# Relative-bias attention and a snake-activation MLP in one kernel: numerators and divisions in two groups per head pair, one transpose of x per pair, other loads and planner figures

## The chip, the cores and the metric

The kernel runs on one core of a Trainium2 chip. A core has a matrix engine (TensorE, PE; its weight loads are shown as PEld), a vector engine (VectorE, DVE), a scalar engine (ScalarE, ACT), GpSimd (POOL) and SyncE (SP), which run separate instruction streams and wait for each other through semaphores, and 16 DMA engines. The metric is the device time of one execution in microseconds.

## The reference

```python
def _attn_ref(q, k, v, bias_table):        # q, k, v: (8, 8, 576, 64); bias_table: (32, 8)
    scores = scale * np.matmul(q, k.transpose(0, 1, 3, 2))
    ...
    bias = bias_table[bucket]              # bucket: a function of |i - j|, 31 from some distance on
    scores = scores + bias.transpose(2, 0, 1)[None, :, :, :]
    scores = scores - np.max(scores, axis=-1, keepdims=True)
    attn = np.exp(scores)
    attn = attn / (np.sum(attn, axis=-1, keepdims=True) + 1e-09)
    return np.matmul(attn, v).astype(np.float32)

def _moe_ref(x, w_in, w_out, alpha):       # x: (4608, 512), w_in: (512, 2048), w_out: (2048, 512)
    h = x @ w_in
    s = np.sin(alpha * h)
    g = h + s * s / (alpha + 1e-09)
    return (g @ w_out).astype(np.float32)

def reference(**kwargs):
    ...
    x = np.ascontiguousarray(attn_out.transpose(0, 2, 1, 3)).reshape(B * S, H * D)
    return _moe_ref(x=x, **moe_kwargs)
```

## The kernel before

**Attention** goes through the 8 sequences t and, in each, the 4 head pairs p. k and q are wanted with the head dimension on the partitions: for t = 0 and 1 they are loaded by rows into the buffer of tile g (`natural`, L259), turned on PE by identity (`turn`, L366) and copied to kT and qT (L396); for later t POOL casts them into HBM (`stage`, L238) and SP's DMA transposes fetch them (L245). kL (L417) holds the last 64 keys of both heads of a pair in the two diagonal corners, so that one matmul with all 128 rows serves both heads. A pair has five score tiles of up to 1024 columns: X (last 64 keys and last 64 queries, L601 and L608) and four of 256 by 256 blocks (L698); one small tile S per sequence serves the last keys against the last queries (L575). ScalarE takes exp of each tile into a u (L544). The bias is a product afterwards: exp(bias - bias at distance 31) stands in m2 and mt, built at the start by selecting table rows with a matmul (`mask`, L459), and DVE multiplies the tiles near the diagonal by it (L616, L618, L709, L713, L717).

**Numerators and divisions.** `av_task` (L626) makes one unit of 128 queries for both heads: 9 matmuls (L639, L643) into 130 columns of one bank of PSUM (tile av), column 64 of each head being the sum of the exps. Three such slots of the bank are used in turn. `norm` then does a reciprocal (L653) and a multiply (L657) per unit into tile xp. A pair has five units; the one of the last 64 queries comes first. `xtr` (L735) turns xp into xT by two DMA transposes on SP (four chunks of 128 rows, then 64 rows).

**The MLP** goes through 9 blocks of 512 tokens. `moe_in(b)` (L747) has 8 steps of 1024 features: 8 matmuls (L764), two sines (L774), a square (L781) and two fused multiply-adds into g (L788); then 16 pieces of 4 matmuls with w_out (L821), an eviction (L837) and a store for each 128 tokens. A block needs xT of all its tokens. Block t - 1 stands behind pair 1 of sequence t, and block 0 behind pair 0 of sequence 1.

**The order** of each engine's instructions is made in advance: `_Plan` (L60) knows tasks with an engine, a duration, a latency, dependencies, rings of buffers and a priority, plays them through and emits them in the order of its clock. HOP is what passes from one engine to another, LATENCY what an engine's result takes, SWITCH what a change of kind costs. The tasks on the ring `big` (score tiles, masks and moe steps, three PSUM buffers) keep the order in which they were added. POOL's loads keep theirs too: k and q of t = 0 (heads 0 and 1, then the other six), v of t = 0, w_in, k and q of t = 1, v, w_out, then the later sequences.

Of the kernel before, what the change touches and what calls it, by code (L numbers as in the profile page):

```python
# [47 lines left out]
class _Task:  # L48
    def __init__(self, eng, dur, emit, deps=(), prio=0, lat=0.0, rings=(), seq=None, name="", mode=None):
        self.eng, self.dur, self.emit = eng, dur, emit  # L50
        self.deps = list(deps)
        self.prio, self.lat, self.rings = prio, lat, list(rings)
        self.mode = mode
        self.seq = seq
        self.name = name
        self.start = None
        self.end = None


class _Plan:  # L60
# [4 lines left out]
    HOP = 0.1  # L65

    LATENCY = {"PE": 0.15, "ACT": 0.1, "DVE": 0.08}
# [19 lines left out]
    def _ready(self, t):  # L87
        r = 0.0
        for d in t.deps:
            if d.end is None:  # L90
                return None
            r = max(r, d.end + self.HOP)
# [11 lines left out]
    def run(self):  # L104
# [9 lines left out]
        while left:  # L114
            moved = False
            nxt = None
            for e, lst in engs.items():
# [13 lines left out]
                if best is not None:  # L131
# [5 lines left out]
                    best.start = now  # L137
# [19 lines left out]
def kernel(  # L157
# [34 lines left out]

    bt = _bucket_table(256)
    cst_np = np.zeros((128, 672), dtype=np.float16)
    for g in range(4):
        for z in range(511 - g):
            cst_np[32 * g + bt[abs(255 - z)], z + g] = 1.0
        cst_np[32 * g:32 * g + 32, 640 + 8 * g:648 + 8 * g] = 1.0
# [10 lines left out]
    xT = sgl.tile([128, NP, NT], F16, name="xT")  # L209
# [5 lines left out]
    t31 = sgl.tile([128, H], F32, name="t31")  # L215
    dtab = sgl.tile([128, H], F32, name="dtab")
# [11 lines left out]
    big, avr, mor = _Ring(3), _Ring(3), _Ring(1)  # L228
# [40 lines left out]

    def load_v(t):  # L270
# [27 lines left out]
    def pre_sp():  # L298
# [3 lines left out]
        nc.sync.dma_start(  # L302
            out=t31, in_=bass.AP(tensor=bias_table.tensor,
                                 offset=bias_table.offset + (NB - 1) * H,
                                 ap=[[0, 128], [1, H]]))
# [31 lines left out]
    def pre_tab():  # L337

        nc.vector.tensor_tensor(out=dtab, in0=tab4, in1=t31, op=ALU.subtract)
        nc.vector.tensor_copy(out=hilo[:, 0, :], in_=dtab)  # L340
        nc.vector.tensor_tensor(out=hilo[:, 1, :], in0=dtab, in1=hilo[:, 0, :], op=ALU.subtract)
# [7 lines left out]
    t_tab = add("SP", 0.9, pre_sp, lat=1.6)  # L349
# [3 lines left out]
    t_al = add("SP", 1.2, pre_sp2, lat=4.0)  # L353
    t_dve0 = add("DVE", 1.5, pre_dve)
    t_bt = add("DVE", 0.7, pre_tab, deps=[t_tab, t_sp0], prio=-3)
    t_alpha = add("DVE", 0.4, pre_alpha, deps=[t_al])
# [9 lines left out]
    def turn(t, p):  # L366

        for kind in range(2):
# [3 lines left out]
            def e_pe(kind=kind, cell=cell, first=first):  # L372
                if first:

                    avs["t"] = ps.tile([128, 512], F32, name="av", tag="av", bufs=1)
                    avs["n"] = 0
                    s = cell["t"] = avs["t"].bitcast(F16)
                else:
                    s = cell["t"] = ps.tile([128, 512], F32, name="mo", tag="mo", bufs=1).bitcast(F16)
                r = nat[t]["n"]  # L380
                for j in range(NL):
# [8 lines left out]
            def e_cp(kind=kind, cell=cell, first=first):  # L390
                dst = (kTs, qTs)[kind][t % 2][:, p, 0:S].rearrange("d (r j) -> d r j", j=NL)
                src = ap(cell["t"], 0, [[1, NR], [NR, NL]])
                if first:
                    nc.scalar.activation(out=dst, in_=src, func=AF.Copy)
                else:
                    nc.vector.tensor_copy(out=dst, in_=src)  # L396
            users = []
            a = add("PE", 0.6, e_pe, deps=[T_nat[t][p][kind], t_sp0], prio=-0.5 if t else -2 if p == 0 else 0,
                    rings=[(avr, users)] * 3 if first else [(mor, users)], mode="full",
                    name=f"turn{t}.{p}.{kind}")  # L400
            if first:
                c = add("ACT", 0.7, e_cp, deps=[a], prio=-1, name=f"turn{t}.{p}.{kind}c")
            else:
                c = add("DVE", 0.6, e_cp, deps=[a], prio=-2, name=f"turn{t}.{p}.{kind}c")
# [3 lines left out]
        corners(t, p, 1, [T_kT[t][p], t_dve0])  # L408

    def corners(t, p, n, deps):  # L410
        def emit():
            for a_ in range(2):
                r = slice(64 * a_, 64 * a_ + 64)
                dst = kLs[t % 2][r, p:p + n, 64 * a_:64 * a_ + 64]
                src = kTs[t % 2][r, p:p + n, 512:576]
                if n == 1:
                    nc.vector.tensor_copy(out=dst, in_=src)  # L417
                else:
                    nc.sync.dma_start(out=dst, in_=src)
        c = add("DVE" if n == 1 else "SP", 0.25 if n == 1 else 0.9, emit, deps=deps, prio=-1,  # L420
                name=f"kL{t}.{p}")
        if n > 1:
            c.lat = 3.0
        T_kL[t][p:p + n] = [c] * n
# [4 lines left out]
    def load_nat(t):  # L429
        kq = ((0, k), (1, q))  # L430

        def one(emit, dur):
            first = not made
            made.append(add("GQ", dur, emit, lat=3.0, seq="GQ",
                            rings=[(gr, nat_users[t])] if first else []))
            return made[-1]
        made = []
        parts = [(0, 2), (2, 6)] if t == 0 else [(0, 8)]
        for h0, n in parts:
            got = [one(natural(src, t, kind, h0, n), 0.45 * n) for kind, src in kq]  # L440
            for p in range(h0 // 2, (h0 + n) // 2):
                T_nat[t][p] = got

    load_nat(0)
    T_v[0] = add("GQ", 5.0, load_v(0), deps=[t_dve0], lat=3.0, seq="GQ")
# [31 lines left out]
    avs = {}  # L477
    T_mt = []

    def masks_tail():  # L480

        for pp in range(2):
            cell = {}

            def g_mm(pp=pp, cell=cell):
                if "t" not in avs:
                    avs["t"] = ps.tile([128, 512], F32, name="av", tag="av", bufs=1)
                    avs["n"] = 0
                cell["t"] = avs["t"][:, 0:384].rearrange("p (a b) -> p a b", a=2)
# [11 lines left out]
            a = add("PE", 0.4, g_mm, deps=list(T_m2), prio=-1, rings=[(avr, users)] * 3,  # L501
# [9 lines left out]
    def later_loads(t):  # L511
        pre_k = last_qk[t - 2] if t >= 2 else []
        pre_v = last_av[t - 2] if t >= 2 else [t_dve0]
        if t == 1:
            for j in range(4):
                T_win.append(add("GQ", 2.5, w_in_load(j), lat=2.0, seq="GQ"))
        if t < TN:
            load_nat(t)
        else:
# [7 lines left out]
            corners(t, 0, NP, [c] + pre_k)  # L527
        T_v[t] = add("GQ", 5.0, load_v(t), deps=pre_v, lat=3.0, seq="GQ")
        if t == 1:
            for i in range(4):  # L530
                T_wout.append(add("GQ", 2.5, w_out_load(i), lat=2.0, seq="GQ"))


    def feed_tile(cell, dur, full, rows, exp_cols, deps_pe, tag, ring=None, kind="u", bufs=NU, home=None):
# [12 lines left out]
        if batch["open"] is not None:  # L547
# [8 lines left out]
        else:  # L556
# [5 lines left out]
        b = add("ACT", 0.05 + exp_cols / 1200.0, e_act, deps=[a], seq="ACT",  # L562
                rings=[(ring or ur, uu)], name=tag + "e", mode="exp")
        users.append(b)
# [5 lines left out]
    def attn_s(t, cell):  # L570
        qT, kL = qTs[t % 2], kLs[t % 2]

        def full(s):
# [3 lines left out]
        a, b = feed_tile(cell, 0.14, full, None, 256, T_kL[t] + T_qT[t], f"S{t}",  # L577
# [13 lines left out]
    def attn_pair(t, p, sc):  # L591
# [12 lines left out]
        def mm_x(s):  # L604
            for c in range(4):
# [5 lines left out]
        ax, bx = feed_tile(cx, 0.36, full_x, mm_x, 1024, kq + [T_kL[t][p]], f"X{t}.{p}")  # L611
# [14 lines left out]
        def av_task(units, part, deps, qc):  # L626


            cell = {}

            def emit():
                if "t" not in avs:
                    avs["t"] = ps.tile([128, 512], F32, name="av", tag="av", bufs=1)
                    avs["n"] = 0
                o = cell["o"] = 130 * (avs["n"] % 3)
                avs["n"] += 1
                av = avs["t"]
                tail, bl = units()
                nc.tensor.matmul(out=av[:, o:o + 130], lhsT=tail, rhs=vt_[:, p, 0:130],  # L639
                                 start=True, stop=True, skip_group_check=True)  # L640
                for a_ in range(2):
                    for c in range(4):
                        nc.tensor.matmul(  # L643
                            out=av[:, o + 65 * a_:o + 65 * a_ + 65],
                            lhsT=bl(a_, c), rhs=vv[:, c, hA + a_, 0:65],
                            start=False, stop=True, skip_group_check=True)

            def norm():
                if "x" not in xcell:
                    xcell["x"] = tp.tile([128, 5, 128], F16, name="xp", tag="xp", bufs=NX)  # L650
                av, x, o = avs["t"], xcell["x"], cell["o"]
                r = tp.tile([128, 2], F32, name="rden", tag="rden", bufs=6)
                nc.vector.reciprocal(  # L653
                    out=r[0:part, 0:2],
                    in_=bass.AP(tensor=av.tensor, offset=av.offset + o + 64,
                                ap=[[av.ap[0][0], part], [65, 2]]))
                nc.vector.tensor_tensor(  # L657
                    out=bass.AP(tensor=x.tensor, offset=x.offset + 128 * qc,
                                ap=[[x.ap[0][0], part], [64, 2], [1, 64]]),
                    in0=bass.AP(tensor=av.tensor, offset=av.offset + o,  # L660
                                ap=[[av.ap[0][0], part], [65, 2], [1, 64]]),
                    in1=bass.AP(tensor=r.tensor, offset=r.offset,
                                ap=[[r.ap[0][0], part], [1, 2], [0, 64]]),
                    op=ALU.mult)
            users = []
            a = add("PE", 0.3, emit, deps=deps + [T_v[t]], prio=1, rings=[(avr, users)],
                    name=f"av{t}.{p}.{qc}", mode="full")
            rings = [(xr, xusers)] if not norm_done else []
            b = add("DVE", 0.4, norm, deps=[a], prio=0, rings=rings, name=f"norm{t}.{p}.{qc}")
# [4 lines left out]
        def units_q4():  # L674
# [3 lines left out]
        a4 = av_task(units_q4, 64, [dx], 4)  # L678
        if "band" in sc:
            a4.deps.append(sc["band"])  # L680
            sc["users"].append(a4)
        else:
            sc["early"].append(a4)
        cx["users"].append(a4)
# [230 lines left out]
```

## Time and profile before

| | us |
|---|---|
| three runs | 430.11, 436.71, 435.34; median 435.34 |
| profiled execution | 435.95, of it the span of the instructions 434.1 |
| mean granted clock | 0.972 |
| PE, DVE, ACT, POOL busy | 386.6, 317.6, 272.9, 74.7 |
| L544 exp, 160 of 128x1024 | 154.7 |
| L764 and L821 matmuls | 134.3 and 132.1 + 15.9 |
| L653 and L657, 160 each | 26.3 and 46.4 |
| L788, L781, L709 | 100.9, 48.9, 43.8 |

All times in views are us from the span's first instruction unless marked ns. A line such as "PE av L639" is an engine, the tile written and the line of the program; "<-" names what ended a wait. A row of the timeline has its start, its length, the engine, the line, the operation, what it writes and reads, and in brackets the idle time before it. In the chain that ended last, PE has 55% of the span and DVE 37%.

### The profile page before, as it was taken

What the parts mean: (1) busy time and instruction counts of PE and PEld (TensorE: products, weight loads), DVE (VectorE), ACT (ScalarE), POOL (GpSimd) and SP (SyncE); (2) the same over time, 40 slices, a digit from 0 to 9 for tenths busy, and PEclk for the clock granted to TensorE, in tenths of its full rate; (3) what the DMA queues carried; (4) which work ended last, traced back from release to release, by engine and by line L of the source; (5) the groups of instructions that cost most, each with busy time, mean ns of one, the idle gap of its engine ahead of it and who ended that gap; (6) DMA issues with size and microseconds to landing.
All of it is one profiled execution on the core that took longest, in us unless ns stands there. A gap on an engine that the chain in (4) does not pass through costs nothing.

```text
span 434.1 us, 9402 instructions
## 1 busy us (share of the span) xinstructions
PE 386.6 (89%) x3848; PEld 206.5 (48%) x3848; DVE 317.6 (73%) x827; ACT 272.9 (63%) x333; POOL 74.7 (17%) x78
## 2 busy tenths in 40 slices
PE   3774778999799899989998999899989999999996
PEld 3653533455345554455445544554455445444442
DVE  4578848877687669866986698768866896399811
ACT  2666516888549784979397948794778486355400
POOL 7526260006100430034003500220000000000000
PEclk9889669999989999999999999999999999999999
DMA  9999999719990799359933994293212101100021
GB/s 117 194 197 171 178 143 154 67 41 107 144 127 31 81 143 113 98 69 156 118 91 55 152 121 107 45 152 63 65 40 53 30 32 40 39 26 0 24 98 73
DMA packets 158463, 40.78 MB, mean 94 GB/s; under 512 B 148052, under 2 KB 153300, under 8 KB 158420
## 3 DMA queue, kind: packets, MB, share of 16 engines
q0 software_dynamic: 98976, 18.35, 54.9%
q1 hardware_dynamic: 59300, 21.66, 26.9%
q8 instruction: 30, 0.49, 0.5%
q10 hardware_dynamic: 144, 0.17, 0.1%
q14 instruction: 13, 0.11, 0.1%
HBM read 36.89 MB, written 16.52 MB: 123 GB/s over the span
## 4 chain that ended last, share of the span: by engine, by line
PE 55%; DVE 37%; issue 4%; DMA 2%; ACT 1%; SPq 0%; DVEq 0%
PE mo L821 17%; DVE g L788 15%; PE big L764 15%; PE av L643 8%; DVE sq L781 7%; PE big L698 5%; DVE xp L657 4%; PE av L639 3%; PE av L821 3%; DVE outs L837 3%; DVE rden L653 2%; DMA xT<-xp 2%; PE big L459 1%; DVE kL L417 1%; PE big L601 1%
## 5 line engine op out<-in xcount | busy, mean ns | idle before, releaser
L544 ACT ACTIVATE u<-big 128x1024 f16<-128x1024 f32 x160 | 154.7, 1022 | 35.2 <-PE big L698 21.7
L774 ACT ACTIVATE s<-big,alphaT 128x512 f16<-128x512 f32 x144 | 90.8, 684 | 87.2 <-PE big L764 87.1
L764 PE MATMUL big<-xT,w_in 128*128 128x512 f16 x576 | 134.3, 387 | 4.8 <-DVE g L788 4.1
L821 PE MATMUL mo<-w_out,g 128*128 128x512 f16 x512 | 132.1, 380 | 6.2 <-DVE g L788 3.5
L788 DVE SCALAR_TENSOR_TENSOR g<-sq,inv_a,big 128x512 f16<-128x512 f16 x144 | 100.9, 744 | 1.7
L764 PEld LDWEIGHTS <-w_in 128*128 128x128 f16 x576 | 57.0, 100 | 74.9 <-issue 11.4
L821 PEld LDWEIGHTS <-g 128*128 128x128 f16 x576 | 50.9, 97 | 67.1 <-issue 10.8
L643 PEld LDWEIGHTS <-u 128*128 128x128 f16 x1280 | 53.3, 99 | 28.8 <-issue 19.8
L781 DVE TENSOR_TENSOR sq<-s 128x1024 f16<-128x1024 f16 x72 | 48.9, 687 | 24.7 <-ACT s L774 24.6
L643 PE MATMUL av<-v,u 128*128 128x65 f16 x1280 | 61.1, 195 | 1.3 <-DVE u L709 1.3
L277 POOL DMA_DIRECT2D v<-in_v_dram x32 | 28.3, 901 | 193.5 <-PE av L643 192.1
L653 DVE RECIPROCAL rden<-av 128x2 f32<-128x2 f32 (+1 forms) x160 | 26.3, 165 | 40.6 <-PE av L643 40.1
L657 DVE TENSOR_TENSOR xp<-av,rden 128x128 f16<-128x128 f32 (+1 forms) x160 | 46.4, 290 | 5.5
L709 DVE TENSOR_TENSOR u<-u,m 128x1024 f16<-128x1024 f16 x64 | 43.8, 684 | 4.9 <-ACT u L544 4.9
L698 PE MATMUL big<-qT,kT 64*128 64x256 f16 x512 | 43.3, 279 | 0.0
L639 PE MATMUL av<-vt,u 128*128 128x130 f16 x128 | 28.7, 224 | 10.0 <-DVE xp L657 9.9
L837 DVE COPY outs<-mo 128x512 f32<-128x512 f32 x32 | 22.0, 687 | 6.8 <-PE mo L821 6.1
L698 PEld LDWEIGHTS <-kT 64*128 64x128 f16 x512 | 19.0, 96 | 16.6 <-issue 13.9
L639 PEld LDWEIGHTS <-u 128*128 128x128 f16 x128 | 12.5, 98 | 9.5 <-issue 3.8
L238 POOL DMA_DIRECT2D staged_q<-in_q_dram x6 | 16.7, 2788 | 0.0
L821 PE MATMUL av<-w_out,g 128*128 128x512 f16 x64 | 15.9, 379 | 0.0
L639 PE MATMUL av<-vt,us 128*128 128x130 f16 x32 | 7.1, 221 | 9.7 <-DVE xp L657 9.4
(56 smaller groups left out, 189.5 us busy)
## 6 DMA issues: line engine op xcount, KB each, us to landing
out_dram<-outs SPq DMA_DIRECT2D x36, 256.0 KB, 2.2
v<-in_v_dram POOLq DMA_DIRECT2D x32, 128.0 KB, 5.6
staged_k<-in_k_dram POOLq DMA_DIRECT2D x6, 576.0 KB, 10.9
staged_q<-in_q_dram POOLq DMA_DIRECT2D x6, 576.0 KB, 17.5
w_in<-in_moe_w_in_dram POOLq DMA_DIRECT2D x4, 512.0 KB, 9.3
w_out<-in_moe_w_out_dram POOLq DMA_DIRECT2D x4, 512.0 KB, 11.4
xT<-xp SPq DMA_TRANSPOSE x64, 4.8
g<-in_k_dram POOLq DMA_DIRECT2D x1, 576.0 KB, 13.5
```

Of the source, the lines that this page charges most:

```text
L544: nc.scalar.activation(out=cell["u"][:, 0:exp_cols], in_=cell["s"][:, 0:exp_cols], func=AF.Exp, scale=0.125)
L639: nc.tensor.matmul(out=av[:, o:o + 130], lhsT=tail, rhs=vt_[:, p, 0:130], start=True, stop=True, skip_group_check=True)
L643: nc.tensor.matmul(out=av[:, o + 65 * a_:o + 65 * a_ + 65], lhsT=bl(a_, c), rhs=vv[:, c, hA + a_, 0:65], start=False, stop=True, skip_grou ...
L657: nc.vector.tensor_tensor(out=bass.AP(tensor=x.tensor, offset=x.offset + 128 * qc, ap=[[x.ap[0][0], part], [64, 2], [1, 64]]), in0=bass.AP ...
L698: nc.tensor.matmul(out=s[:, 512 * a_ + 256 * ci:512 * a_ + 256 * ci + 256], lhsT=kT[r, p, 128 * c:128 * c + 128], rhs=qT[r, p, 256 * w:256 ...
L709: nc.vector.tensor_tensor(out=io, in0=io, in1=m2[:, hA:hA + 2, :], op=ALU.mult)
L764: nc.tensor.matmul(out=cell["h"][:, 512 * i:512 * i + 512], lhsT=w_in16[:, j, 128 * f:128 * f + 128], rhs=xT[:, j, 512 * b:512 * b + 512], ...
L774: nc.scalar.activation(out=cell["s"][:, 512 * i:512 * i + 512], in_=cell["h"][:, 512 * i:512 * i + 512], func=AF.Sin, scale=alphaT[:, f:f ...
L781: nc.vector.tensor_tensor(out=cell["sq"], in0=cell["s"], in1=cell["s"], op=ALU.mult)
L788: nc.vector.scalar_tensor_tensor(out=gcell["g"][:, f, :], in0=cell["sq"][:, 512 * i:512 * i + 512], scalar=inv_a[:, f:f + 1], in1=cell["h" ...
L821: nc.tensor.matmul(out=cell["mo"][:, :], lhsT=gcell["g"][:, f, 128 * a_:128 * a_ + 128], rhs=w_out16[:, f, :], start=(f == 0), stop=(f == ...
L837: nc.vector.tensor_copy(out=cell["o"], in_=cell["mo"][:, :])
```

## The change

Numerators: the units of a pair go in two groups, two units and three (the last 64 queries now with the third and fourth chunk). A group has the whole bank; one reciprocal and one multiply divide it, over all 128 partitions. The ring of three slots becomes a ring of one. x of a pair is turned by one DMA transpose of five chunks, whose last 64 columns, of no meaning, are written over by the next sequence; xT is 64 columns longer.

For t = 0 and 1 kL is no longer made: X and S multiply half the rows at a time. For t = 1, k and q come by 128 rows of the sequence (ten loads in place of two, in runs of 64 elements where there were 384), with five transposes each and a copy in order. For t = 0 the loads are by one, one and two pairs. The selection matrix subtracts row 31 itself, so the table is loaded once and not subtracted. Alpha is loaded after the masks. In sequence 1 block 0 of the MLP stands behind pair 1, and w_in is loaded after k and q. The planner's figures change, an instruction on the same engine no longer waits for the latency, and the exp behind the first of two score tiles issued together is planned from the end of that tile.

```diff
-    HOP = 0.1
-    LATENCY = {"PE": 0.15, "ACT": 0.1, "DVE": 0.08}
+    HOP = 0.04
+    LATENCY = {"PE": 0.17, "ACT": 0.1, "DVE": 0.08}
...
-            r = max(r, d.end + self.HOP)
+            if d.eng == t.eng and d.eng in self.LATENCY:
+                r = max(r, d.start + d.took)
+            else:
+                r = max(r, (d.start + t.after[d] if d in t.after else d.end) + self.HOP)
...
-            cst_np[32 * g + bt[abs(255 - z)], z + g] = 1.0
+            cst_np[32 * g + bt[abs(255 - z)], z + g] += 1.0
+            cst_np[32 * g + NB - 1, z + g] -= 1.0
...
+    def natural_chunk(src, t, kind, c):
+        def emit():
+            nc.gpsimd.dma_start(
+                out=rows_of(t)[:, 5 * kind + c, :].rearrange("p (h d) -> p h d", d=D),
+                in_=bass.AP(tensor=src.tensor, offset=src.offset + t * H * S * D + 128 * c * D,
+                            ap=[[D, 128], [S * D, H], [1, D]]))
...
-        nc.sync.dma_start(
-            out=t31, in_=bass.AP(tensor=bias_table.tensor,
...
-        nc.vector.tensor_tensor(out=dtab, in0=tab4, in1=t31, op=ALU.subtract)
-        nc.vector.tensor_copy(out=hilo[:, 0, :], in_=dtab)
+        nc.vector.tensor_copy(out=hilo[:, 0, :], in_=tab4)
...
+                if t:
+                    for c in range(5):
+                        n = 128 if c < 4 else 64
+                        nc.tensor.transpose(out=s[:, 128 * c:128 * c + n],
+                                            in_=r[0:n, 5 * kind + c, 128 * p:128 * p + 128],
+                                            identity=i_sb[0:n, 0:n])
+                    return
...
-        corners(t, p, 1, [T_kT[t][p], t_dve0])
...
-        parts = [(0, 2), (2, 6)] if t == 0 else [(0, 8)]
+            for h0, n, lat in ((0, 2, 4.0), (2, 2, 5.0), (4, 4, 6.0)):
...
+            got = [[one(natural_tail(src, t, kind), 0.7, 4.0)] for kind, src in kq]
+            for kind, src in kq:
+                got[kind] += [one(natural_chunk(src, t, kind, c), 0.9, 5.0) for c in range(4)]
...
+    t_al = add("SP", 0.5, pre_sp2, deps=T_m2, lat=6.0)
...
+        for load in ((kqs, w_ins, v_s, w_outs) if t == 1 else (kqs, v_s)):
+            load()
...
+        b = add("ACT", 0.92 if exp_cols == 1024 else 0.42, e_act, deps=[a], seq="ACT",
+        if first:
+            b.after[a] = dur + 0.27
...
+            if t < TN:
+                for w in range(2):
+                    for a_ in range(2):
+                        r = slice(64 * a_, 64 * a_ + 64)
+                        nc.tensor.matmul(out=s[r, 512 * w + 256:512 * w + 512],
+                                         lhsT=kT[r, p, 512:576],
+                                         rhs=qT[r, p, 256 * w:256 * w + 256],
+                                         start=True, stop=True)
...
-                r = tp.tile([128, 2], F32, name="rden", tag="rden", bufs=6)
+                r = tp.tile([128, 6], F32, name="rden", tag="rden", bufs=4)
+                nc.vector.reciprocal(out=r[:, 0:2 * n], in_=ap(av, 64, [[65, 2 * n]]))
                 nc.vector.tensor_tensor(
+                    out=ap(x, 128 * q0, [[64, 2 * n], [1, 64]]),
+                    in0=ap(av, 0, [[65, 2 * n], [1, 64]]),
+                    in1=ap(r, 0, [[1, 2 * n], [0, 64]]), op=ALU.mult)
...
-            a = add("PE", 0.3, emit, deps=deps + [T_v[t]], prio=1, rings=[(avr, users)],
+            a = add("PE", 0.29 * n, emit, deps=deps + [T_v[t]], prio=1, rings=[(avr, users)],
...
             nc.sync.dma_start_transpose(
-                out=xT[:, p, n0:n0 + 512].rearrange("d (c s) -> d c s", c=4),
-                in_=x[:, 0:4, :].rearrange("s c d -> s (c d)"))
-            nc.sync.dma_start_transpose(out=xT[:, p, n0 + 512:n0 + 576], in_=x[0:64, 4, :])
+                out=xT[:, p, n0:n0 + 640].rearrange("d (c s) -> d c s", c=5),
+                in_=x[:, 0:5, :].rearrange("s c d -> s (c d)"))
...
-            if p == (0 if t == 1 else 1) and t >= 1:
+            if p == (1 if t == 1 else 1) and t >= 1:
                 moe_in(t - 1)
```

## The prediction

> **What bounds the kernel now.** I read the slices of the page first, then the busy time in chosen windows, then the timeline where an engine stood still, then the waits of TensorE.
>
> ```profile
> PE   3774778999799899989998999899989999999996
> DVE  4578848877687669866986698768866896399811
> PEclk9889669999989999999999999999999999999999
> DMA  9999999719990799359933994293212101100021
> ```
> From the ninth slice (87 us) on PE is near full at full clock. Before it PE is the emptiest, the clock drops to 0.6 and the DMA engines are full. So there are two kernels to price: a start and a repeating middle.
>
> ```profile
> core 0: us, PE busy (x) PEld busy (x) DVE busy (x) ACT busy (x) POOL busy (x), PEclk, DMA share, GB/s
> 199.30:243.70 44.40, 41.90 (x418) 22.02 (x416) 34.62 (x93) 32.42 (x41) 9.25 (x9) 1.00 1.01 106
> ...
> 252.00:267.20 15.20, 14.61 (x81) 6.33 (x79) 14.57 (x24) 9.35 (x13) 0.00 (x0) 1.00 1.00 120
> 267.20:288.10 20.90, 19.52 (x275) 11.57 (x272) 15.22 (x56) 17.07 (x20) 4.79 (x6) 1.00 0.69 82
> ```
> The chain of waits shows the same step coming back every 44.4 us (the first 24 matmuls of a moe block, L764, at 199.3, 243.7, 288.1, 332.5 us): four head pairs plus one 512-token block. PE is idle for 2.5 of 44.4 us. Within it 15 us are held by DVE as much as by PE (14.57 of 15.20), and 21 us by PE alone. Hence nothing done to DVE can give more than 2.5 us a period here.
>
> ```profile
> PE av L639 <- DVE xp L657: 4.9, 12, 0.6
> PE mo L821 <- DVE g L788: 1.8, 6, 0.3
> PE mo L821 <- DVE outs L837: 0.7, 3, 0.2
> ```
> These are PE's waits over three such periods (199.3 to 332.5 us; total, times, longest): 1.6 us a period are waits of numerator matmuls for a division of an earlier unit.
>
> ```profile
> 37.13 2.21 POOL L238 DMA_DIRECT2D staged_k<-in_k_dram  x1 [0.81 <-DMA v<-in_v_dram]
> ...
> 38.10 3.65 DVE L417 COPY kL<-kT 64x64 f16<-64x64 f16 x2
> ...
> 38.84 2.72 POOL L238 DMA_DIRECT2D staged_q<-in_q_dram  x1
> ...
> 42.32 0.22 PE L639 MATMUL av<-vt,us 128*128 128x130 f16 x1 [3.97 <-DVE xp L657]
> ```
> A 178 ns copy lasts 3.46 us and ends at 41.57, with the end of the two POOL issues; PE stands still for 3.97 us, and from 43.2 to 50.0 us its granted clock is 0.50. The other such copy (54.02, 0.46 us) also ends with a POOL issue.
>
> **The start, part by part.** Before, ScalarE's first score tile starts at 16.11 us; five pairs are through when the moe block 0 starts (57.8 us, held until 59.82 by the transpose of x that was issued at 53.07), and moe block 1 starts at 109.28.
>
> *Table.* DVE waits until 5.59 for t31, the second table load. The packets of tab4, the first, end at 3.12, so the masks on PE can start up to 2 us before 6.54; a DVE subtract (0.2 us) goes too. PE then lost 1.91 us at 13.3 to "issue", which no edit touches. Against it, the m2 copy (L474, 0.42 us, at 9.75, when POOL was between issues) now falls among back-to-back POOL issues; by the two held kL copies that costs 0.3 to 3.3 us. I take 1 us gained, from 1 lost to 4 gained.
>
> *kL copies.* 16 × 178 ns = 2.85 us and the two holds of 3.29 + 0.28 us leave DVE's stream. The matmuls that used kL become twice as many of half the rows, like those of L608 that go in pairs (8 in 0.22 us): nothing on PE.
>
> The Trainium skill (SBUF — State Buffer, Who interferes with whom) says that a copy in a two-port mode and a GpSimd operation shut each other out for a whole instruction, and that a tensor_tensor does not suffer from descriptor writing. The trace agrees on the second point: 64 band multiplies (L709) last 672 to 694 ns, POOL busy or not. By that rule the m2 copy would be held for one POOL issue, 0.9 us at most; the copy at 38.10 outlasted one.
>
> *Divisions.* A unit now costs DVE 0.41 us from start to start (L653 to L657 0.20, to the next 0.21), a pair 2.05 us. Two groups: two reciprocals at 0.20, a multiply of 256 and one of 384 elements. A 128x384 read from PSUM takes 0.555 us (L498), 128x128 takes 0.292 (L657), so 256 takes 0.42; less the 0.08 by which followers overlap, 0.34 + 0.47. Sum 1.21, a saving of 0.84 us a pair.
>
> *Copies of the t=1 turn.* 8 × 0.75 us with a scattered order. In straight order I bound them by 0.75 (no change) and 0.46 (0.51 ns an element, as the 1024-element multiply has); I take 0.55, 1.6 us less. Five transposes for twelve take some 0.2 us less a time on a PE that waits anyway.
>
> *Who limits six pairs.* The changed code puts moe block 0 behind t=1's second pair, so six pairs come first. DVE: bands 6 × 1.87 (0.60, 0.60, 0.20, 0.20, 0.13, 0.14, start to start), divisions 6 × 1.21, remaining copies 6 × 0.67 and 8 × 0.5, rest 1.5: 28 us. ACT: 30 tiles at 0.97 (154.7 us / 160), 1.4 of others: 30.5 us. ACT becomes the longest. It ran full for ten tiles from 16.11 and 82% full in the middle's PE-bound part (17.07 of 20.90). Between 30.5 and 37 us I take 34: block 0 starts at 15.1 + 34 = 49 us, with one pair more done than before.
>
> *Loads.* w_in behind t=1's k and q, and those in runs of 64 elements instead of 384. t=1's k and q now land 5.7 us after w_in (27.3 to 33.0); v, in the same short runs and half as many packets, took 4.0 (13.2 to 17.2) and 5.0 us (33.0 to 38.0), so 8 to 10: everything behind comes 2.4 to 4.4 us later. k and q land near 26, w_in near 36, v near 41, w_out near 53, all ahead of use. What is tight is t=2: kT and qT landed at 69.1 and 75.2, kL at 76.6, now about 80. Two pairs and a moe block after 49 us they are wanted at about 49 + 17 + 10 = 76. PE has the block's output matmuls (13.8 us) to run meanwhile. I take 2 us, 0 to 6. POOL's ten issues (8 × 0.9 + 2 × 0.7 = 8.6 us for 1.6) stay ahead of the engines.
>
> The Trainium skill (DMA: Bandwidth & Descriptors, Why small descriptors are slow) counts 11 cycles for 8 at 256 bytes; by it the short runs would add some 1.3 us instead of 2.4 to 4.4, with the same answer for what is tight.
>
> *Sum of the start.* From block 0 to block 1 there are four pairs and one block, a whole period: 44.4, less nothing. 49 + 44.4 + 2 = 95.4 for 109.28: 13.9 us gained. Bounds: 6 (six pairs at 37 us, DMA late by 6, 1 lost at the table) and 20.
>
> **The middle and the end.** Six periods to moe block 7. DVE falls by 4 × 0.84 = 3.4 us a period, most of it where PE rules. In the DVE-ruled stretch four divisions (249.8 to 252.1, 4 × 0.41 = 1.64) become two groups (1.21): 0.4 us. The waits for a division (1.6 us) come from three slots of one bank that are reused unit by unit; now one group owns the bank, and the next group waits for its whole division, 0.54 or 0.67 us behind any band or moe step on DVE. Queued behind that wait on PE is all that follows in its stream, but score tiles and output pieces (0.86 each) can lie between. I take 0.6 us a period gained, from 1.5 gained to 1.0 lost: 3.6 us in six. x's single transpose saves SP 32 issues of 1.2 us; at the end two output pieces cover the last landing (372.4 against PE until 372.9), so nothing. The last two blocks (373 to 434 us) are PE's and unchanged. Alpha, now loaded behind the masks, is first read by L788 in block 0, long after; the planner's new figures add no instruction, only reorder, and get nothing.
>
> Together 13.9 + 3.6 = 17.5: span 434.1 → 416.6. The profiled run took 435.95, 1.85 more than its span and 0.6 over the median, so 418.
>
> **Rivals.** *The loads rule the start.* If six pairs take 37 us and t=2 arrives 10 us late (88 instead of 76.6, when short packets cost their full time: 9,216 × 33 ns / 16 for 1,536 × 80 ns / 16 is 11.3 us more), block 1 starts near 104: 5 us gained, 427 to 430. For: the DMA slices are full to 79 us. Against: between 50 and 60 us the trace has 10,970 short packets, twice that rate, so they overlap. *ACT fills and the middle tightens.* Six pairs in 31 us and 1.4 us a period: 434 − 19 − 8, 408. *The single bank rules.* Of the 48 groups in t=2 to 7 each waits uncovered for its division (0.6 on average) and for what DVE has in front (0.4), less the 1.6 × 6 of today: 38 us lost, against 13.9 gained: 458. Slower by 2% begins at about 0.46 us more wait for a group. Against: a pair has 5.2 us of PE time (20.90 / 4) and its two divisions last 1.21. *The plan's new figures only reorder*, start and middle as before: 432.
>
> **Numbers.** Forecast 418: 0.58. ACT-full 408: 0.15. Loads 428: 0.12. Reorder only: 0.05. Single bank: 0.10. The forecast's own bounds are 410 and 428; the range 406 to 431 leaves out the single bank, the last rival and little else. 2% (8.7 us) is about what a measurement can tell from no change: faster 0.58 + 0.15 + a third of the loads = 0.77; within 0.13; slower 0.10.
>
> **What would show it.** Moe block 0 near 49 us and block 1 near 95; no DVE copy over 1 us behind POOL; clock 0.5 for less than today's 20 us before 64; L657 at 64 instructions of 0.42 and 0.55 us; waits of L639's successor for xp under 1.6 us a period; a period of 43.8. A period over 46, or block 1 after 104, makes the forecast wrong.

## The result and the profile after

The changed kernel takes 406.42 us (median of 4 runs, 405.6 to 406.78) beside 433.94 us of the kernel before on the same chip: a ratio of 0.939, 95% interval 0.932 to 0.946. The forecast was 418, with bounds of its own of 410 to 428 and a range of 406 to 431: the time lies below those bounds and 0.4 us inside the edge of the range. The profiled execution took 406.59 us with a span of 404.6, against 434.1: 29.5 us less, where 17.5 had been summed. First the slices of the changed kernel's page:

```profile
PE   6788599989999999999999999999999998999996
DVE  4587469666976698659956896779666964699811
PEclk9699899999999999999999999999999999999999
DMA  9999999999933998199919991981021103000121
```

PE is near full from the sixth slice (51 us) instead of the ninth. The time at half clock in the start fell from about 20 us to 10: the windows 10 to 20 and 40 to 50 us have a mean of 0.66 and 0.83, so 6.8 + 3.4 us at 0.5. The DMA engines are now busy 90% or more for 111 us on end, before for 76. Next the stretch from moe block 3 to moe block 4 (first matmuls of L800), to be held against 199.3 to 243.7 before:

```profile
core 0: us, PE busy (x) PEld busy (x) DVE busy (x) ACT busy (x) POOL busy (x), PEclk, DMA share, GB/s
177.47:219.58 42.11, 41.10 (x418) 22.16 (x416) 32.26 (x70) 31.99 (x40) 9.23 (x9) 1.00 1.13 113
```

The period is 42.11 instead of 44.38 us. PE's idle time fell from 2.5 to 1.0 us, and PE's *busy* time too, from 41.88 to 41.10, with the same work. PE's waits over three such periods (177.5 to 304.1 us; total, times, longest):

```profile
PE mo L857 <- DVE outs L873: 2.5, 9, 0.3
PE av L680 <- DVE xp L695: 0.5, 3, 0.2
PE big L800 <- DMA xT<-xp: 0.2, 1, 0.2
```

The wait of numerators for a division, 4.9 us before, is 0.5. The divisions themselves, the group of L695 with its two shapes (minimum, median, maximum in ns):

```profile
L695 DVE TENSOR_TENSOR xp<-av,rden x64: 423/491/559, 22.9 to 339.8; 128x256 f16<-128x256 f32 x32, 128x384 f16<-128x384 f32 x32
```

Where the 29.5 us came from, by the starts of the moe blocks:

| stretch | before | after | gained | forecast |
|---|---|---|---|---|
| to block 0 (one pair more after) | 57.79 | 49.30 | 8.49 | 8.8 |
| block 0 to 1 | 51.33 | 43.27 | 8.06 | 5.1 |
| block 1 to 7 (six periods) | 263.82 | 252.05 | 11.77 | 3.6 |
| block 7 to the end | 61.2 | 60.0 | 1.2 | 0 |

The start was close; the middle gave three times what it was given. 1.3 of its 11.77 us have another cause: before, block 1's period held a stretch at half clock (118.3 to 121.7 us, 0.50). The four periods after it gained 2.03 each, and the stretch from block 6 to 7 only 0.08.

### The profile page after: what moved, and what is told of

The parts are those of the page before. It is cut to its first block, busy times and chain, and to the rows that moved or that the text cites. A ratio compares the mean times of both kernels' runs of the same rounds, so it can differ in the third digit from the quotient of the medians.

```text
span 404.6 us, 9103 instructions
## 1 busy us (share of the span) xinstructions
PE 375.5 (93%) x3816; PEld 202.9 (50%) x3816; DVE 289.5 (72%) x618; ACT 270.1 (67%) x333; POOL 82.6 (20%) x88
## 4 chain that ended last, share of the span: by engine, by line
PE 49%; DVE 25%; DMA 11%; ACT 10%; issue 5%; SPq 0%; POOL 0%; ACTq 0%; DVEq 0%; POOLq 0%
PE mo L857 20%; DVE g L824 11%; PE big L800 11%; DMA xT<-xp 8%; ACT u L567 7%; DVE sq L817 5%; PE av L684 5%; PE big L725 3%; PE av L857 3%; DVE outs L873 3%; DVE xp L695 2%; ACT s L810 2%; DMA kL<-kT 2%; DVE u L736 2%; PE av L680 1%
## 5 line engine op out<-in xcount | busy, mean ns | idle before, releaser
L800 PE MATMUL big<-xT,w_in 128*128 128x512 f16 x576 | 132.1, 379 | 1.9 <-DMA xT<-xp 1.2
L857 PE MATMUL mo<-w_out,g 128*128 128x512 f16 x512 | 127.6, 380 | 6.7 <-DVE outs L873 6.0
L800 PEld LDWEIGHTS <-w_in 128*128 128x128 f16 x576 | 55.8, 98 | 69.1 <-issue 4.3
L817 DVE TENSOR_TENSOR sq<-s 128x1024 f16<-128x1024 f16 x72 | 49.3, 684 | 15.9 <-ACT s L810 15.9
L684 PE MATMUL av<-v,u 128*128 128x65 f16 x1280 | 55.4, 194 | 0.0
L684 PEld LDWEIGHTS <-u 128*128 128x128 f16 x1280 | 50.9, 98 | 4.1
L695 DVE TENSOR_TENSOR xp<-av,rden 128x256 f16<-128x256 f32 (+1 forms) x64 | 31.4, 491 | 3.8 <-DMA xT<-xp 1.6
L725 PEld LDWEIGHTS <-kT 64*128 64x128 f16 x512 | 19.8, 96 | 13.4 <-issue 10.5
L680 PEld LDWEIGHTS <-u 128*128 128x128 f16 x128 | 12.4, 97 | 15.6 <-DVE xp L695 6.1
L694 DVE RECIPROCAL rden<-av 128x4 f32<-128x4 f32 (+1 forms) x64 | 11.8, 184 | 11.9 <-PE av L684 11.8
L744 DVE TENSOR_TENSOR u<-u,m 128x256 f16<-128x256 f16 x32 | 9.3, 290 | 14.9 <-ACT u L567 14.9
L857 PE MATMUL av<-w_out,g 128*128 128x512 f16 x64 | 14.5, 379 | 0.0
```

The lines of the kernel that those rows point to most:

```text
L684: nc.tensor.matmul(out=av[:, o + 65 * a_:o + 65 * a_ + 65], lhsT=bl(a_, c), rhs=vv[:, c, hA + a_, 0:65], start=False, stop=True, skip_grou ...
L695: nc.vector.tensor_tensor(out=ap(x, 128 * q0, [[64, 2 * n], [1, 64]]), in0=ap(av, 0, [[65, 2 * n], [1, 64]]), in1=ap(r, 0, [[1, 2 * n], [0 ...
L725: nc.tensor.matmul(out=s[:, 512 * a_ + 256 * ci:512 * a_ + 256 * ci + 256], lhsT=kT[r, p, 128 * c:128 * c + 128], rhs=qT[r, p, 256 * w:256 ...
L800: nc.tensor.matmul(out=cell["h"][:, 512 * i:512 * i + 512], lhsT=w_in16[:, j, 128 * f:128 * f + 128], rhs=xT[:, j, 512 * b:512 * b + 512], ...
L817: nc.vector.tensor_tensor(out=cell["sq"], in0=cell["s"], in1=cell["s"], op=ALU.mult)
L857: nc.tensor.matmul(out=cell["mo"][:, :], lhsT=gcell["g"][:, f, 128 * a_:128 * a_ + 128], rhs=w_out16[:, f, :], start=(f == 0), stop=(f == ...
```

## The experiments

Two theories for the middle: the *groups* (TensorE starts less often behind a division; VectorE has less to do) or the planner's *figures* (same instructions, better order). For the start: kL copies, the order and form of the loads, the place of block 0. Each run stands beside fresh runs of the kernel before; "period" is from one block's first matmul to the next between blocks 2 and 6.

**The groups alone**, put into the kernel before; nothing else of the change.

```diff
-big, avr, mor = _Ring(3), _Ring(3), _Ring(1)     # before.py
+big, avr, mor = _Ring(3), _Ring(1), _Ring(1)
...
-        a4 = av_task(units_q4, 64, [dx], 4)      # and a task for each unit
...
+            av = av_task(units, bands + [dx], 2 * w)
```

> The kernel before with only the numerators and divisions in two groups a pair (and the bank held by one group at a time). If the grouping alone shortens the middle: periods 44.4 to about 42.3, time about 434 - 6 x 2.1 - 1 = 420 us. If the figures do it: periods stay at 44.4, the time is 432 to 435 us. If a single bank for a whole group makes TensorE wait, as one of my rivals had it, periods rise over 45 and the time goes over 440 us.

409.98 us, ratio 0.946 (0.939 to 0.954). Period 41.65, which is shorter than in the whole change; block 0 at 49.02, block 1 at 99.00. The groups alone bring most of the gain, in the start too: 10.1 of the 16.55 us by block 1, where I had expected 1 us, which is why the time is 10 us under my 420. PE's waits for divisions up to 60 us are half of what they were (total, times, longest; the kernel before, then the groups alone):

```profile
PE av L639 <- DVE xp L657: 8.8, 9, 4.0
PE av L633 <- DVE xp L648: 4.5, 3, 3.0
```

The corner copies kL are all still there, and the longest lasts 490 ns instead of 3464 (minimum, median, maximum in ns):

```profile
L415 DVE COPY kL<-kT x16: 166/176/490, 10.2 to 50.9; 64x64 f16<-64x64 f16 x16
```

In this order none of them lies beside a staging issue, so the hold that cost PE 3.97 us is gone although the copies are not.

**The figures alone taken back** (the rule for one engine and `after` too), and **both taken back** (units as in the next diff).

```diff
-    HOP = 0.04
+    HOP = 0.1
-    LATENCY = {"PE": 0.17, "ACT": 0.1, "DVE": 0.08}
+    LATENCY = {"PE": 0.15, "ACT": 0.1, "DVE": 0.08}
...
-        b = add("ACT", 0.92 if exp_cols == 1024 else 0.42, e_act, ...
+        b = add("ACT", 0.05 + exp_cols / 1200.0, e_act, ...
```

> The changed kernel planned with the figures of before (a hand-over of 0.1 us, also on the same engine, and the old latency of TensorE and duration of the exponential); it runs the same instructions in another order. If the grouping made the middle shorter: periods stay near 42.2, the time is 406 to 410 us. If the planner's figures did: periods go to about 44.2, the time to about 406.4 + 6 x 2.1 = 419 us. My prediction gave the figures nothing; by it this run is at 406.

> Both taken back: five divisions a pair and the old figures of the planner, with the changed loads, table, corner products and turn of x. What is left of the gain is then the start's: periods of about 44.3 as before, block 1 near 94 to 96 (92.6 in the changed kernel, 109.1 before), time about 434 - 14 = 420 us whichever of grouping and figures shortened the middle. If the middle's gain came from neither of the two (from the single turn of x or the corner products), periods stay under 42.8 and the time is under 411 us.

408.87 us (0.945, 0.935 to 0.955) with periods of 42.48: the figures are worth 2.5 us at most (the two intervals overlap), in the middle 0.4 a period at most. The profiled spans differ by 1.4 us, of which 1.3 lie behind the start of block 7. With both gone 436.54 us (1.007, 1.002 to 1.012), periods of 46.50: my expectation of 420 missed. The starts of numerators cost it no more than the kernel before (4.57 and 4.89 us a period, table below); the 2.1 us a period that it is slower lie elsewhere, and I take them for its order, which no run shows. Against the run with the groups and the same old figures it is 4.0 us a period slower. Its block 1 starts at 97.83, so the edits other than groups and figures are worth up to 11.3 us there, the groups 10.1, and all together 16.55: they overlap.

**Units with the new figures.**

```diff
...
-            av = av_task(units, bands + [dx], 2 * w)
+            for i, one_unit in enumerate(units):
+                av = av_task([one_unit], bands + [dx], 2 * w + i)
...
-                st = add("DVE", 0.66, e_stt(i), deps=[sq, t_alpha], prio=0.4,
+                st = add("DVE", 0.66, e_stt(i), deps=[sq, t_alpha] + stts[:1], prio=0.4,
```

> The changed kernel, new planner figures and all, with five divisions a pair in three slots of the bank (and the first of a block's multiply-adds made to come first, which changes no instruction order in the changed kernel). Grouping theory: the 20 starts of a unit's numerators in a period cost about 2.9 us more on TensorE, as between the kernel before (4.9 us for 20) and the grouped one (2.0), so periods of 44.5 to 46.5, block 1 at 95 to 98, 423 to 434 us. Figures theory: the new figures make up for most of it, periods under 43, 407 to 411 us.

467.41 us (1.074, 1.068 to 1.080), periods of 47.0 to 51.1: both expected ranges missed. With the runs above, the figures theory falls: the groups gain with the old figures, and with units the new figures and the last line of this diff make an order that is 31 us slower than the old figures made. How much of the 31 is that line's, no run separates; without it, units and new figures make an order that deadlocks.

**Grouped numerators, divisions unit by unit.**

```diff
-                nc.vector.reciprocal(out=r[:, 0:2 * n], in_=ap(av, 64, [[65, 2 * n]]))
...
+                for i in range(n):
+                    nc.vector.reciprocal(out=r[:, 2 * i:2 * i + 2], in_=ap(av, 130 * i + 64, [[65, 2]]))
...
```

> The changed kernel with TensorE's numerators in two groups a pair as changed, but VectorE's division of a group done unit by unit again, five reciprocals and five multiplies of 128 elements a pair, all behind the group's last numerator; plan and order as changed. If the grouping pays because TensorE no longer starts a unit's numerators behind a division (20 starts cost 4.9 us a period before and about 2.0 with groups), periods stay at 42.1 to 42.6, block 0 comes 0 to 3 us later, time 406 to 411 us. If it pays because VectorE is freed of 0.84 us a pair, that time comes back: 3.4 us a period, periods of 44 to 45.5, time 418 to 428 us.

416.91 us (0.960, 0.951 to 0.968), periods of 43.61, between the two expectations. The plan's order is that of the change, so in this order 1.5 us a period is what VectorE's relief is worth by itself (seven of them are the 10.5 us between the two times); 0.4 of it lies in the starts of numerators (table below). Its DVE is busy 34.94 of 43.60 us, as busy as before. PE's waits over three of its periods (141.8 to 272.6 us) show where it is lost, at hand-overs from DVE, most of them not the division's:

```profile
PE mo L858 <- DVE outs L874: 4.0, 9, 0.6
PE av L680 <- DVE xp L696: 1.3, 3, 0.4
PE big L801 <- DVE g L825: 1.0, 3, 0.4
```

**Why the groups gave more than the waits showed.** Two timelines of PE: in the kernel before, the last two units of a pair and the first of the next; with the groups alone, the last three of a pair (start, us, operation, idle before it and its releaser).

```profile
234.42 0.23 PE L639 MATMUL av<-vt,u 128*128 128x130 f16 x1
234.49 0.40 PE L643 MATMUL av<-v,u 128*128 128x65 f16 x8
234.73 0.22 PE L639 MATMUL av<-vt,u 128*128 128x130 f16 x1
234.79 0.40 PE L643 MATMUL av<-v,u 128*128 128x65 f16 x8
235.79 0.22 PE L639 MATMUL av<-vt,us 128*128 128x130 f16 x1 [0.60 <-DVE xp L657]
```

```profile
215.30 0.23 PE L633 MATMUL av<-vt,u 128*128 128x130 f16 x1
215.37 0.41 PE L637 MATMUL av<-v,u 128*128 128x65 f16 x8
215.61 0.22 PE L633 MATMUL av<-vt,u 128*128 128x130 f16 x1
215.67 0.40 PE L637 MATMUL av<-v,u 128*128 128x65 f16 x8
215.91 0.22 PE L633 MATMUL av<-vt,us 128*128 128x130 f16 x1
```

Undisturbed, units start 0.30 us apart. Before, the third started 1.06 us after the second: 0.76 lost, of which the profile calls 0.60 idle. The other 0.16 counts as PE busy, because the matmuls in front are shown until their modelled end, 0.16 us past the point at which the next could have started. So a wait under some 0.16 us need not be shown at all, and a longer one is shown short. I therefore added up, over three periods, the time from the matmul in front of a unit to the unit's first matmul (20 such starts a period):

| kernel | period | the 20 starts | all else |
|---|---|---|---|
| before | 44.38 | 4.89 | 39.49 |
| groups alone | 41.65 | 2.01 | 39.64 |
| changed | 42.20 | 2.12 | 40.08 |
| figures back | 42.48 | 2.01 | 40.47 |
| both back | 46.50 | 4.57 | 41.93 |
| divisions by unit | 43.60 | 2.52 | 41.08 |

From before to groups alone the starts explain 2.88 us against 2.73 measured. The profile's idle for them was 1.6. The same sum up to block 0 is 13.0 us before (24 starts) and 6.7 with the groups alone (22), so most of the 8.8 us that block 0 gains there is of the same kind. In the last row the rest of the period rose by 1.0 too: VectorE's work also delays what PE wants from it elsewhere.

**kL copies back.**

```diff
+        T_kL[t][p] = add("DVE", 0.25, e_kl, deps=[T_kT[t][p], t_dve0], prio=-1, ...
-                           kq + ([T_kL[t][p]] if t >= TN else []), ...
+                           kq + [T_kL[t][p]], ...
```

> The changed kernel with the corner copies kL for the first two sequences back on VectorE (16 of 178 ns, 2.85 us) and the products that read them as full-row matmuls; loads, order and figures as changed. My prediction: copies held behind POOL's issues, of which the changed kernel has 26 in the first 29 us (7.4 of every 10 us), so the eight copies of sequence 0 at 14 to 24 us and some of sequence 1 last 0.5 to 3.5 us instead of 0.18; block 0 comes 3 to 7 us later (52 to 56 us), time 409 to 413 us. Rival: ScalarE or the loads set the pace of the start and the copies lie beside them: block 0 within 1 us of 49.3, time 406 to 407.5 us.

406.58 us (0.933, 0.928 to 0.937): no cost that can be measured. In the profiled execution, with 407.61 us the slowest of four, block 0 starts at 50.87 and block 1 at 94.65, 1.6 and 2.1 us later, and the middle, which had two longer periods in the changed kernel's, took back 0.9. No copy was held long, beside 30 POOL issues of up to 1 us in the first 29 us (minimum, median, maximum in ns):

```profile
L432 DVE COPY kL<-kT x16: 173/179/618, 7.2 to 41.1; 64x64 f16<-64x64 f16 x16
```

**k and q of sequence 1 in long runs**, the plan kept.

```diff
-            got = [[one(natural_tail(src, t, kind), 0.7, 4.0)] for kind, src in kq]
+            got = [[one(natural(src, t, kind, 0, 8), 0.7, 4.0)] for kind, src in kq]
```

> The changed kernel with k and q of sequence 1 loaded as before (two loads in runs of 384 elements) and turned by twelve transposes with a scattered copy a time; the plan's order is kept. What it costs by my prediction: eight copies of 0.75 instead of 0.45 us and eight times 0.2 us on TensorE. Rival, that the loads set the start: the short runs delay v of sequence 1, whose last piece lands at 45.6 us and for which TensorE stands still 3.96 us (41.8 to 45.8); with long runs v lands 3 to 5 us earlier, that wait falls under 1 us, and block 0 starts at 46 to 48 us, the time is 403 to 405 us. If the copies outweigh it: block 0 at 50 to 52 us, 407 to 409 us.

406.45 us (0.932, 0.928 to 0.937). v landed at 39.5 instead of 45.6 us and block 0 started at 44.71, but then it stood 4.5 us for the fourth turn of x (issued at 40.03, landed at 49.95), and block 1 came at 92.89: the wait was only moved.

**Block 0 behind the first pair of sequence 1** (and the multiply-adds of a block ordered as in the run with units).

```diff
-            if p == (1 if t == 1 else 1) and t >= 1:
+            if p == (0 if t == 1 else 1) and t >= 1:
```

> The changed kernel with moe block 0 placed behind the first pair of sequence 1, as before, instead of the second; planned again with the new figures. If the later place is worth something in the start (block 0 needs x's fourth transpose of sequence 0, which the kernel before waited 2 us for at 57.8 us): block 0 starts at about 45 to 50 us but block 1 is 1 to 4 us later than 92.6 us, time 408 to 411 us. If not: block 1 within 1 us of 92.6 and the time 405 to 408 us. The middle is not touched except by the order that the plan falls into (period 42.1 to 43).

442.64 us (1.016, 1.011 to 1.020). Block 1 is 4 us later, and the rest is the plan's: periods of 44.3 to 45.8, and 16 us more behind the start of block 8, where 240 matmuls are left to do instead of 184. PE's waits over three periods (187.4 to 321.3 us):

```profile
PE mo L857 <- DVE outs L873: 7.1, 5, 2.3
PE big L725 <- DVE g L824: 2.9, 2, 1.4
```

This is a second case of an order that the new figures, with the same line on the multiply-adds, make badly (the units' run also has 240 matmuls behind block 8), so it cannot price block 0's place.

**Taking the start apart: four candidates.** w_out's loads held on POOL until the last pair of sequence 0 is divided, and five buffers of x, with the long runs; or instead with v ahead of w_in. A load is held by a small copy on POOL that reads the awaited tile; what POOL issues afterwards waits with it:

```diff
+            if i == 0:
+                nc.gpsimd.tensor_copy(out=junk[:, 0:2], in_=xlast[3][:, 4, 0:2])
             nc.gpsimd.dma_start(out=w_out16[:, 4 * i:4 * i + 4, :], ...
```

> A candidate: the changed kernel with k and q of sequence 1 in runs of 384 (block 0 then started at 44.7 us but stood 4.5 us for the fourth turn of x, issued at 40.0 and landed at 49.95 among the loads of w_out), with w_out's loads held on POOL until the last pair of sequence 0 is divided, and five buffers of x instead of three. If the backlog of loads is what holds the turn of x: it lands 3 to 6 us earlier, block 0 no longer waits for it, block 1 starts at 88 to 91 us, time 401 to 405 us. If what holds block 1 is the k and q of sequence 2 (landing at 73 and 81 us) or VectorE and ScalarE, block 1 stays at 92 to 93 us and the time at 405 to 407 us.

> A candidate: the changed kernel with v of sequence 1 loaded before w_in instead of behind it, w_out held until the last pair of sequence 0 is divided, five buffers of x. TensorE's wait of 3.96 us for v at 41.8 us should go (v lands before 40 us); w_in then lands near 42 us, before block 0 wants it. If that wait is on the path: block 0 at 45 to 47 us, block 1 2 to 4 us earlier, time 402 to 405 us. If block 1 waits for the loads of sequence 2, it stays at 92 to 93 us, time 405 to 407 us.

407.12 and 406.41 us (0.939, 0.931 to 0.948; 0.936, 0.929 to 0.943). Block 0 starts at 43.42 and 44.40 us, x's fourth turn lands at 44.24 and 46.34, and the gain is lost again before block 1, at 91.71 and 93.31. In the first of the two the wait of PE between 43 and 95 us is now

```profile
PE big L614 <- DMA kL<-kT: 5.2, 1, 5.2
```

The k and q of sequence 2, turned by DMA from 59.96 to 78.4 us, rule it (kL landed at 79.8). So v of sequence 2 and the staging of sequence 3 were held too:

```diff
+            if t == 2:
+                nc.gpsimd.tensor_copy(out=junk[:, 0:2], in_=kTs[0][:, 0, 0:2])
             for c in range(4):       # load_v
```

> A candidate on top of the one with runs of 384, w_out held and five buffers of x, which only moved the wait: block 0 at 43.4 us, but then TensorE stood 5.2 us for kL of sequence 2, whose k and q were turned from 60 to 79.8 us, while v of sequence 2 and the staged rows of sequence 3 (issued from 45 and 60 us) shared the DMA engines. Here POOL holds those two until k of sequence 2 has been turned (about 66 us). If that traffic is what makes the turns late: kL lands at 74 to 76 us, the wait falls under 1.5 us, block 1 at 87 to 89 us, time 400.5 to 403 us. If the turns are slow by themselves or v now comes too late (wanted near 85 us): block 1 at 91 to 93 us, 405 to 408 us.

> The same, and the staging of k and q of sequence 2 moved ahead of w_out's loads on POOL (issued near 27 instead of 42 us, landing by about 50 instead of 60 and 65 us); w_out then lands at 55 to 60 us and is wanted from about 58 us on. If the staging was what the turns of sequence 2 waited for: kL lands by 72 us, no wait for it, block 1 at 86 to 89 us, time 400 to 403 us. Against it: the fourth turn of x (issued at 38.7, landed at 44.2 us) gets the staging in its way and w_out comes late; then block 0 is back at 47 to 50 us or its output matmuls wait 1 to 5 us, and the time is 404 to 409 us.

**399.49 us** (ratio 0.923, 0.919 to 0.928, 6 runs): it beats both kernels. The two turns take 60.0 to 69.7 instead of 78.4 us, kL lands at 72.4, PE no longer waits for it, and block 1 starts at 84.99. Which of the two held transfers mattered, no run separates. SP's issues of the two turns, without and with the hold:

```profile
59.96 5.55 SPq L249 DMA_TRANSPOSE kT<-staged_k  x1
65.62 6.44 SPq L249 DMA_TRANSPOSE qT<-staged_q  x1
60.02 4.80 SPq L250 DMA_TRANSPOSE kT<-staged_k  x1
64.92 2.71 SPq L250 DMA_TRANSPOSE qT<-staged_q  x1
```

Moving the staging ahead of w_out as well gave 401.86 us (0.928, 0.923 to 0.933). In its profiled execution, at 404.44 us the slowest of six, x's fourth turn lands at 48.7, PE waits 2.6 us for it, and block 1 comes at 91.03. The slices of the best one:

```profile
PE   6688898999999999999999999999999999999996
DMA  9999999999949990799329981980210103000122
```

## Why the prediction was right, and where it was not

The direction, the size of the start's gain and the fall of the single-bank rival were right. The sum was 12 us short: 8.2 of these are one term, the middle, and 3.0 are block 0 to 1, mostly the same term once more. That the time still lies in the range, by 0.4 us, is luck: the forecast's own bounds of 410 to 428 missed it, and only the range, which takes in the rival at 408, reaches down so far.

- **The middle, 0.6 us a period (from 1.5 gained to 1.0 lost): the step that failed.** 2.0 to 2.3 were gained in the change, 2.73 by the groups alone. "PE is idle for 2.5 of 44.4 us … Hence nothing done to DVE can give more than 2.5 us a period" took the profile's idle time for all that waits cost. The divisions' waits cost 2.9, not the 1.6 shown, and grouping removed nearly all of them instead of trading them for others: a group waits 0.5 us in three periods. VectorE's relief alone is worth 1.5 a period (divisions by unit against the change), where I had 0.4 from one stretch; the waits of output pieces and moe blocks for DVE fall with it. The Trainium skill (Perfetto Trace Analysis, Identifying the Most-Contended Engine) advises against matmul busy time as the measure of what is left, and for the busy share of the weight loads: that is 22.02 of 44.38 us before (50%) and 21.88 of 41.65 with the groups alone (53%), with PE at 94% and 99%. So that share left room where busy PE seemed to leave none, without a price for it. It says that matmuls look smaller than they are; in these records the 512-element ones are drawn longer, 380 ns at a pitch of 216 (L800 of the changed kernel). The row with the groups alone, to be held against 199.30 to 243.70 before:

```profile
181.79:223.44 41.65, 41.12 (x418) 21.88 (x417) 32.06 (x70) 32.19 (x40) 9.23 (x10) 1.00 1.11 113
```

- **Divisions.** 0.42 and 0.56 us for the predicted 0.42 and 0.55, 0.18 and 0.19 for the reciprocals. DVE is 2.4 us a period less busy, where I had 3.4.
- **Block 0 near 49 us: the number was right by luck, its reason was not.** The groups alone, with the old loads and the kL copies, have it at 49.02 too, though with a pair less done. I had ScalarE at 34 us for six pairs. With the loads rearranged (the run of 399.49 us) block 0 starts at 43.7 us, 29.7 us behind the first score tile (14.04), so ScalarE's 30.5 was near the truth, and loads held the rest. v of sequence 1 landed at 45.6 us where I had 41, and PE stood for it (timeline of the changed kernel):

```profile
41.42 0.39 PE L725 MATMUL big<-qT,kT 64*128 64x256 f16 x4 [0.34 <-ACT u L567]
45.77 0.24 PE L680 MATMUL av<-vt,u 128*128 128x130 f16 x1 [3.96 <-DMA vt<-in_v_dram]
```

- **The short runs,** priced at 2.4 to 4.4 us. Against long runs, k and q landed 2.4 us later, w_in 3.1 and v 6.2. The prediction's second estimate, 1.3 us, should by its own cycles be 1.7 (66 for six short runs, 51 for a long one), and is low as well.
- **Block 0 to block 1.** The whole period of 44.4 that I carried over from the middle was itself too long by the same term; 43.27 was measured, with 1.2 us of waiting for kL (landed at 82.1; I had about 80 and 2 us).
- **kL copies.** 2.85 us of work and 3.57 of holds were named, but the sum went by ScalarE's 34 us, so they had no price of their own; they are worth 2 us at block 1 in one execution and nothing measurable in the time. The long hold lay beside two staging issues of over 2 us; the issues of rows and weights held a copy for 0.4 us at most, and in the two other runs that have these copies none lay beside a staging issue, so no run tried the long hold again.
- **Table and masks.** 1 us taken, 1.6 gained; the first score tile starts at 14.47 instead of 16.11. The 0.4 us copy of m2 (L491) was not held although POOL was issuing; alpha's TENSOR_SCALAR was, 0.59 us instead of 0.21; it ends at 7.94 together with the second of the three POOL issues (7.00 to 7.94):

```profile
6.13 2.68 POOL L298 DMA_DIRECT2D v<-in_v_dram  x3
...
7.02 0.42 DVE L491 COPY m<-m 128x1024 f16<-128x1024 f16 x1
...
7.35 0.59 DVE L351 TENSOR_SCALAR tmp_a<-alphaT 128x16 f32<-128x16 f32 x1
```

  The Trainium skill (SBUF — State Buffer, Who interferes with whom) lets a copy or a tensor_scalar be blocked for a whole instruction when GpSimd has issued first. Here one was held and one not, so it names a risk and no price.
- **The other copies of t = 1** last 0.45 us, the lower bound, where 0.55 was taken.
- **The figures** "get nothing": 2.5 us here at most. But the reason, that they only reorder, hid a risk: with units, the new figures and the line on the multiply-adds were 31 us slower. I had no rival for that.
- **The rivals.** *The loads rule the start* was wrong as a price, since the start gained 16.55, and right as a mechanism: it is what separates 406.4 from 399.5. *ACT fills and the middle tightens* (408, given 0.15) came nearest, with 2.0 instead of 1.4 a period, but its block 0 was at 46 us (15.1 + 31) and not at 49.3.

What stays open: which part of the rest makes the changed kernel's period 0.5 us longer than that of the groups alone. The table puts 0.44 into "all else"; no run separates the single turn of x from the order that the plan fell into.

## What to carry to other kernels

The idle time that these profiles show for TensorE is a lower bound on what hand-overs cost (1.6 shown, 2.9 lost), because matmuls in flight are drawn as busy: count the starts behind another engine and compare each with the same start undisturbed. Where one engine waits for small results of another, fewer and larger hand-overs can pay twice, in the waits and in the other engine's work; here the second alone was worth 1.5 us a period. A planner's figures can make a good order for one set of work and one 31 or 36 us slower for a set that differs little, as they did here, so after any edit of the work read the order again. And when one transfer stops being late, look at once which is late next: here v, x's turn and the turns of sequence 2 share the DMA engines, and only the third edit paid.

## Not expected of the hardware

Two turns by DMA of a staged sequence took 18.4 us (59.96 to 78.4) while v and the next staging shared the DMA engines, and 9.7 us (60.0 to 69.7) with those held back, although the bytes are the same; the kT issue itself occupied its queue for 5.6 and 4.8 us, the qT issue for 6.4 and 2.7. The turn of one pair's x issued before 45 us took from 4.6 us (39.04 to 43.59, the run of 399.49 us) to 13.2 us (29.16 to 42.37, the run with v ahead of w_in) from issue to landing, and its issue alone up to 5.0 us (that run, at 31.11).
